# Two attention layers on one core: sums begun a unit earlier, six raw blocks in the last products, and outgoing tiles moved to band columns

## The chip, the core and the metric

The kernel runs on one core of one Trainium2 chip. A core has a matrix engine (TensorE; PE in the profile, with its weight loads shown apart as PEld), VectorE (DVE), ScalarE (ACT), GpSimd (POOL) and SyncE (SP), which here only issues DMAs. Each engine works through its own instruction list in order and waits for the others by semaphores. The matrix engine writes to PSUM; VectorE and ScalarE read PSUM and SBUF; transfers between the large memory (HBM) and SBUF run on sixteen DMA engines, and are issued here by SP, ACT and POOL. The metric is the device time of one execution in microseconds (us), lower is better.

## The reference

Two independent attention layers, each with 2048 positions of width 1024, 32 heads of 32, and fp32 inputs; the two outputs stand side by side.

```python
def _A_ref(x, wqkv, wo):          # layer A: 8 keys per query, every second position
    W, dil = 8, 2
    ...
    idx = pos[:, None] - (jnp.arange(W) * dil)[None, :]
    logits = einsum("bhsd,bhswd->bhsw", q, k[idx]) * scale     # masked where idx < 0
    o = einsum("bhsw,bhswd->bhsd", softmax(logits), v[idx])
    return o.reshape(B, S, D) @ wo

def _B_ref(x, wqkv, wo):          # layer B: a sliding window of 256 keys
    mask = (i - j >= 0) & (i - j < 256)
    o = softmax(where(mask, q @ k.T * scale, -1e9)) @ v
    return o.reshape(B, S, D) @ wo

out = concatenate([_A_ref(...), _B_ref(...)], axis=-1)
```

## The kernel before

**Units.** The work is cut into eight units of 512 positions. Units 0 to 3 are layer B, units 4 to 7 layer A ("the first to the fourth unit of layer A"; the odd and even positions of layer A are laid apart first, so its window is eight neighbours). A unit has eight head groups `s` of four heads; `hg = 8 * unit + s` numbers them through, so layer A has 32 to 63. For each head group the gemm of queries and keys runs (`qk_items`, L577), in some groups a block of the value gemm (`v_items`, L645), then the attention itself: in layer A `window`, with its scores (L914), a chain of mask, maximum, exponential and sum on DVE and ACT, a transposition (L952) into columns 1024 and up of a tile `band`, copies of those into a tile `wide` on ACT (L961, L964), and the product with the values (L975). There are two `band` tiles, taken by `hg` even and odd. `finish` copies the result to an SBUF slot and, in layer A, SP stores it to a DRAM tile `od` (L1028).

**fp32 through three products.** The matrix engine takes operands split in two parts, high and low. A block of 128 x 1024 floats (512 KB) arrives in a *raw* tile by a DMA that POOL issues (L169); ACT (L213) or DVE (L216) copies the high part out, DVE subtracts for the low part (L219); each 128 x 128 x 512 product then takes three matmuls.

**The stream of blocks.** `Stream` holds all blocks that are to be loaded, x and weights, in the order of their use (`items`). There are three raw tiles (`NRAW = 3`). When block `i` has been split, its raw tile is free and `load_to(i + 4)` asks for what lies up to three blocks ahead of the next. Some items have a *gate*: a test, in the planned time, that data which must exist first (`od`, `sd`, `td`, below) has been stored.

**The last products.** The output product of layer A isn't done unit by unit. Units 4 and 5, and 6 and 7, are two pairs, and each pair is multiplied with `wo` in seven products instead of eight (a Strassen-like scheme; the table `PRODUCTS`). All fourteen stand at the end of the gemm list (`product`, L764, 48 matmuls each: four groups `n` of twelve). A product needs two x-like blocks and two weight blocks, 512 KB each: some are `od` and `wo` themselves, others are sums, prepared ahead by `background` tasks: `weight_sums` makes `td` out of `wo`, and `output_sums(u, k)` makes `sd[u]` out of `od[u]` and `od[u + 1]`, in four tasks `k` for each pair. A task is two loads of 512 KB on SP's queue (L832), four additions on DVE (L837) and two stores of 512 KB on SP's queue (L843); it holds one of two lanes of SBUF slots. In the kernel before, the tasks of a pair are begun when head groups 4 to 7 of its second unit (unit 5, unit 7) have been stored. The product's additions out of PSUM are on DVE (L782), and its outputs are stored by ACT's queue (L787). The tile `o` that the second and the fifth product of a pair (`i` 1 and 4) send out is one of two room slots, the same as those that `finish` uses, or the tile `ost`.

**What sets the order.** While the program is being written, a small model (`Clock`) keeps the time at which each engine, queue and transfer would be done. A loop picks, from four lists (attention steps and gemm steps), the step that would be ready first, and writes it; deferred actions (evacuations, splits, loads, tasks) are written when the modelled time passes theirs. So every engine's list is fixed in that planned order, and a task that is begun at another place also shifts the modelled times of what comes after. SP's list has, in that order, the copies of layer A's queries and keys into their *seats* (`by_head`, L497: eight copies a head group, from a tile `nat` of a pool of three into one of two seats), the `od` stores and the tasks' loads and stores. The seats of `hg` are what its scores wait for; the model adds 4.0 us of slack to them (`SEAT_LATE`).

The functions that the diff touches, and what calls them:

Of the kernel before, what the change touches and what calls it, by code (L numbers as in the profile page):

```python
# [7 lines left out]
F32 = mybir.dt.float32  # L8
F32R = mybir.dt.float32r
# [5 lines left out]
P = 128  # L15
# [120 lines left out]
class Stream:  # L136
# [3 lines left out]
    def __init__(self, nc, ck, raws, wpool, xpool, items, more, light):  # L140

        self.nc, self.ck, self.raws, self.wpool, self.xpool, self.more = nc, ck, raws, wpool, xpool, more
        self.items = items
        self.raw, self.tiles, self.ready = {}, {}, {}
        self.loaded = self.split = self.wanted = 0
        self.gates = {}
        self.light = light
        self.load_to(NRAW + len(more))

    def load_to(self, n):  # L150
        while not self.loaded:
            self.raw = {i: (self.raws.tile([P, 1024], F32, tag="raw", name="raw"), []) for i in range(2)}
            for h in range(2):
                for i in range(2):
                    raw, t = self.raw[i]
                    ap = self.items[i][1]
                    self.nc.scalar.dma_start(raw[:, S * h:S * h + S], ap[:, h] if len(ap.shape) == 3 else ap[:, S * h:S * h + S])
                    t.append(self.ck.load("half", self.ck.now))
            self.loaded = 2
        self.wanted = max(self.wanted, n)  # L160
        while self.loaded < min(n, len(self.items)):
            gate = self.gates.get(self.loaded)
            if gate and not gate():
                return
            k = self.loaded - NRAW
            raw = self.more[k] if 0 <= k < len(self.more) else self.raws.tile([P, 1024], F32, tag="raw", name="raw")
            ap = self.items[self.loaded][1]
            early = k < len(self.more)
            (self.nc.scalar if early else self.nc.gpsimd).dma_start(raw if len(ap.shape) == 2 else raw.rearrange("p (a b) -> p a b", a=2), ap)  # L169
            self.raw[self.loaded] = raw, (self.ck.load if early else self.ck.fetch)("load", self.ck.now)  # L170
            self.loaded += 1

    def split_to(self, n):
        while not self.split:
            (rx, tx), (rw, tw) = self.raw.pop(0), self.raw.pop(1)
            self.tiles[0], self.ready[0], self.ready[1] = [], [], []
            w = self.tiles[1] = self.wpool.tile([P, 2, 1024], F32R, tag="w", name="w")
            for h in range(2):
                c = slice(h * S, h * S + S)
                self.tiles[0].append(self.xpool.tile([P, 2, S], F32R, tag="x", name="x"))  # L180
                self.ready[0].append(self.parts(self.tiles[0][h], rx[:, c], tx[h], True))
                self.ready[1].append(self.parts(w[:, :, c], rw[:, c], tw[h], True))
            self.split = 2
            for i in range(2):
                self.ck.defer(self.ready[i][1], lambda n=i + len(self.more) + NRAW + 1: self.load_to(n))
        while self.split < min(n, len(self.items)):
            i = self.split
            self.load_to(i + 1)
            if i not in self.raw:
                return  # L190
            raw, t0 = self.raw.pop(i)
            if self.items[i][0] != "w":
                self.tiles[i], self.ready[i] = [], []
                for h in range(2):
                    t = self.xpool.tile([P, 2, S], F32R, tag="x", name="x") if self.items[i][0] != "xw" else self.sums()
                    self.ready[i].append(self.parts(t, raw[:, h * S:(h + 1) * S], t0, i < SIDE))
                    self.tiles[i].append(t)
            else:
                t = self.wpool.tile([P, 2, 1024], F32R, tag="w", name="w")
                self.ready[i] = self.parts(t, raw, t0, i < SIDE)  # L200
                self.tiles[i] = t
            self.split += 1
            end = self.ready[i] if self.items[i][0] == "w" else max(self.ready[i])
            m = len(self.more)
            self.ck.defer(end, lambda n=i + m + NRAW + 1 if i < NRAW else max(2 * NRAW + m, i + NRAW + 1): self.load_to(n))

    def parts(self, t, raw, t0, side):

# [20 lines left out]
def kernel(ctx, tc, xs, wqk, wv, wo, outs, units):  # L229
# [51 lines left out]
    def landed(key, *which):  # L281
        return lambda: all(done[key].get(w, ck.now + 1) <= ck.now for w in which)
# [71 lines left out]
    def slot(i):  # L354
        return roomp.tile([P, 1024], F32, tag=f"r{i % NO}", name="r")
# [3 lines left out]
        return slot(4 + where_o["s"] % 4).rearrange("p (a s) -> p a s", a=2).bitcast(F32R)  # L359

    st.sums = sums_tile
    qst = [stackp.tile([P, 4, S], F32R, tag=f"q{i}", name=f"qst{i}") for i in range(2)]
    kst = [stackp.tile([P, 4, 256 + S], F32R, tag=f"k{i}", name=f"kst{i}") for i in range(2)]

# [47 lines left out]
    tails = const.tile([P, NG, 8], F32, name="tails")  # L412
    seats = more[:, :2 * (2 * S + 8)].rearrange("p (b c) -> p b c", b=2)
    band, wide = [None, None], [None, None]
    last_dense = sum(NG for u in units if u[2]) - 1
    halo = [[dram.tile([P, 2, 256], F32, name=f"halo{i}_{s}") for s in range(NG)] for i in range(2)]

    xt, xready, ot, rows, waiting = {}, {}, {}, {}, {}
# [315 lines left out]
    def product(u, i):  # L734
# [38 lines left out]
        def after(n, k):  # L773
            if k < 3:
                return
            ps, bank = h["ps"], h["b"]
            if i == 0 and n % 2 == 0:
                h["ac", n // 2] = [slot(8 + 2 * g + n // 2) for g in range(2)]
            a, c = [t[:, S * (n % 2):S * (n % 2) + S] for t in h["ac", n // 2]]

            def add(dst, src):
                nc.vector.tensor_tensor(dst, ps, src, op=ALU.add)  # L782
                return ck.use("dve", 0.61, ck.now + ck.SEM)

            def store(r, col, tile, e):
                def go():
                    nc.scalar.dma_start(outs[ORDER[u + r], 4 * col + n], tile)  # L787
                    ck.load("store", e)
                ck.defer(e, go)

            if i in (1, 4):
                where_o["ot"] += 1
                o = slot(2 + where_o["ot"] % 2)[:, :S] if where_o["ot"] % 3 else stp.tile([P, S], F32, tag="ost", name="ost")
            if i == 0:
                nc.scalar.copy(a, ps)
                e = ck.use("act", 0.485, ck.now + ck.SEM)
            elif i == 1:
                e = add(o, a)
                store(0, 0, o, e)
            elif i == 2:  # L800
                e = add(a, a)
            elif i == 3:
                e = add(c, a)
            elif i == 4:
                e = add(o, c)
                store(1, 0, o, e)
            elif i == 5:
                e = add(c, c)
                store(1, 1, c, e)
                e = add(a, a)  # L810
            else:
                e = add(a, a)
                store(0, 1, a, e)
            rg.give(bank, e)
# [53 lines left out]
    def output_sums(u, k):  # L868
        task([(2 * r, od[u + r][:, k::4, :]) for r in range(2)],
             ((3, 2, 3, ALU.add), (2, 0, 2, ALU.subtract), (0, 3, 0, ALU.subtract), (1, 1, 0, ALU.subtract)),  # L870
             sd[u][:, :, k, :], "s", (u, k))
# [146 lines left out]
    def finish(u, s, h):  # L1018
        hg = u * NG + s
        done["o"][hg] = ck.now  # L1020
        if u >= DU:
            o = slot(2 + hg % 2)[:, :S]
            nc.scalar.copy(o, h["o"])
            e = ck.use("act", 0.485, ck.now + ck.SEM)
            ro.give(0, e)

            def store():
                nc.sync.dma_start(od[u][:, s, :], o)  # L1028
                e2 = ck.copy("store", e)

                def end():
                    done["ot"][hg] = ck.now
                    st.load_to(st.wanted)
                    if s >= 4 and u % 2:
                        output_sums(u - 1, s - 4)

                ck.defer(e2 + 1.0, end)

            ck.defer(e, store)
            return  # L1040
        o = slot(hg).rearrange("p (a s) -> p a s", a=2).bitcast(F32R)
        ot[u, s] = o
        nc.scalar.copy(o[:, 0, :], h["o"])  # L1043
        r = ck.use("act", 0.485, ck.now + ck.SEM)

        def low():
            nc.vector.tensor_tensor(o[:, 1, :], h["o"], o[:, 0, :].bitcast(F32), op=ALU.subtract)  # L1047
            e = ck.use("dve", 0.61, r)
            ro.give(0, e)
            done["ot"][hg] = e  # L1050

        ck.defer(r, low)
# [292 lines left out]
```

## Time and profile before

| | |
|---|---|
| three runs | 1830.73 us median (1830.16 to 1833.35) |
| the profiled execution's own time | 1835.97 us |
| its span, from first to last instruction | 1834.0 us |
| mean granted TensorE clock | 0.991 |
| PE busy | 1799.3 us (98%) |
| DVE, ACT, POOL busy | 1262.2 (69%), 925.6 (50%), 409.2 us (22%) |
| matmuls of the last products (L764) | 672, 159.2 us busy, from 1662.6 us to the end |
| HBM read, written | 189.79 MB, 44.04 MB |

The page gives busy time by engine, the span in 40 slices, the DMA queues, the chain that ended last, and groups of instructions by line: a group's row has its busy time, the mean ns of one instruction, the idle time of the engine just before such instructions, and what ended most of that. In the order of time, a row has a start in us, a duration, engine, line, and in brackets the idle time before it and its releaser. SPq is SP's queue of instructions that issue DMAs. A table by stretches gives, for each window of the span, the busy us of each engine with the number of instructions, the granted clock (1.00 is full speed), the share of time in which the 16 DMA engines were busy, and GB/s.

### The profile page before, as it was taken

What the parts mean: (1) busy time and instruction counts of PE and PEld (TensorE: products, weight loads), DVE (VectorE), ACT (ScalarE), POOL (GpSimd) and SP (SyncE); (2) the same over time, 40 slices, a digit from 0 to 9 for tenths busy, and PEclk for the clock granted to TensorE, in tenths of its full rate; (3) what the DMA queues carried; (4) which work ended last, traced back from release to release, by engine and by line L of the source; (5) the groups of instructions that cost most, each with busy time, mean ns of one, the idle gap of its engine ahead of it and who ended that gap; (6) DMA issues with size and microseconds to landing.
All of it is one profiled execution on the core that took longest, in us unless ns stands there. A gap on an engine that the chain in (4) does not pass through costs nothing. (4 is left out here: it accounts for less than half of the span.)

```text
span 1834.0 us, 38630 instructions
## 1 busy us (share of the span) xinstructions
PE 1799.3 (98%) x14730; PEld 1467.6 (80%) x14730; DVE 1262.2 (69%) x2789; ACT 925.6 (50%) x2302; POOL 409.2 (22%) x950
## 2 busy tenths in 40 slices
PE   9999999999999999999999999999989999999999
PEld 7787777888778888777887788888868888787777
DVE  6777876778867669777777565655765665657666
ACT  4556466565656655656555344533533543435343
POOL 2312323223242323332233200110010011001111
PEclk9999999999999999999999999999989999999999
DMA  8455655645655556455554344547775455347886
GB/s 240 114 146 135 180 164 143 176 121 153 170 151 163 140 151 182 125 155 144 141 141 130 110 148 131 156 144 251 239 230 165 127 159 159 123 153 252 263 251 197
DMA packets 129241, 303.61 MB, mean 166 GB/s; under 512 B 16160, under 2 KB 31520, under 8 KB 129056
## 3 DMA queue, kind: packets, MB, share of 16 engines
q0 software_dynamic: 45216, 164.65, 30.6%
q1 hardware_dynamic: 73472, 116.56, 22.6%
q10 hardware_dynamic: 10368, 19.93, 3.0%
q8 instruction: 117, 1.92, 0.5%
q14 instruction: 68, 0.56, 0.1%
HBM read 189.79 MB, written 44.04 MB: 127 GB/s over the span
## 5 line engine op out<-in xcount | busy, mean ns | idle before, releaser
L577 PE MATMUL g<-x,w 128*128 128x512 f32 x3072 | 774.2, 396 | 6.2 <-ACT x L213 2.0
L577 PEld LDWEIGHTS g<-x,w 128*128 128x128 f32 x3072 | 567.2, 189 | 118.7 <-issue 6.8
L219 DVE TENSOR_TENSOR w<-raw,w 128x512 fp32r<-128x512 f32 x518 | 339.9, 698 | 87.7 <-ACT w L213 80.9
L645 PE MATMUL g<-w,x 128*128 128x256 f32 (+1 forms) x2304 | 396.6, 323 | 0.5 <-issue 0.3
L645 PEld LDWEIGHTS g<-w,x 128*128 128x128 f32 x2304 | 337.0, 192 | 29.6 <-issue 1.4
L1088 ACT ACTIVATE s<-s,nm 128x384 f32<-128x384 f32 (+2 forms) x512 | 274.4, 537 | 102.5 <-DVE nm L1083 102.3
L1083 DVE CUSTOM_DVE_ANT_0 s<-s,mask_d 128x384 f32<-128x384 f32 (+2 forms) x512 | 261.8, 554 | 88.2 <-PE s L1078 87.6
L1147 POOL TENSOR_SCALAR_AFFINE_SELECT pbuf<-pbuf 128x128 f32<-128x128 f32 (+1 forms) x606 | 219.3, 390 | 327.1 <-ACT pbuf L1168 325.8
L1168 ACT ACTIVATE pbuf<-s 128x384 f32<-128x384 f32 (+2 forms) x480 | 202.8, 505 | 73.9 <-PE s L1161 71.7
L705 PE MATMUL g<-r,w 128*128 128x512 f32 x768 | 190.8, 394 | 1.4 <-ACT r L1043 0.7
L169 POOL DMA_DIRECT2D raw<-wqk x126 | 68.2, 541 | 442.0 <-DVE w L219 296.9
L764 PE MATMUL g<-x,w 128*128 128x512 f32 x672 | 159.2, 397 | 7.5 <-ACT w L213 6.4
L705 PEld LDWEIGHTS g<-r,w 128*128 128x128 f32 x768 | 141.9, 188 | 30.8 <-DVE r L1047 1.6
L764 PEld LDWEIGHTS g<-x,w 128*128 128x128 f32 x672 | 127.2, 191 | 39.0 <-ACT w L213 8.1
L1161 PEld LDWEIGHTS s<-qst,kst 128*128 128x128 f32 x704 | 113.2, 189 | 40.9 <-ACT s L1088 16.2
L1078 PE MATMUL s<-kst,qst 96*128 96x384 f32 (+2 forms) x512 | 142.5, 342 | 1.0 <-ACT s L1088 0.7
L216 DVE CAST w<-raw 128x1024 fp32r<-128x1024 f32 x186 | 128.4, 691 | 21.6 <-PE g L577 17.6
L1161 PE MATMUL s<-qst,kst 128*128 128x256 f32 (+2 forms) x704 | 136.5, 302 | 3.5 <-ACT s L1088 3.0
L1078 PEld LDWEIGHTS s<-kst,qst 96*128 96x128 f32 x512 | 93.4, 188 | 26.1 <-issue 4.3
L922 DVE TENSOR_TENSOR band<-s,near 128x160 f32<-128x160 f32 x128 | 32.5, 317 | 111.1 <-PE s L914 111.1
L213 ACT CAST w<-raw 128x1024 fp32r<-128x1024 f32 (+1 forms) x74 | 76.4, 1037 | 61.6 <-DMA raw<-wo 22.8
L1088 ACT ACTIVATION_READ_ACCUMULATOR s<-s,nm 128x1 f32 x512 | 105.3, 206 | 0.0
(80 smaller groups left out, 1409.2 us busy)
## 6 DMA issues: line engine op xcount, KB each, us to landing
raw<-wqk POOLq DMA_DIRECT2D x126, 512.0 KB, 4.4
raw<-wv POOLq DMA_DIRECT2D x72, 512.0 KB, 4.9
qst<-nat SPq DMA_DIRECT2D x96, 256.0 KB, 4.8
kst<-nat SPq DMA_DIRECT2D x96, 256.0 KB, 5.7
raw<-wo POOLq DMA_DIRECT2D x44, 512.0 KB, 4.4
raw<-xs POOLq DMA_DIRECT2D x28, 512.0 KB, 4.7
outs<-ost ACTq DMA_DIRECT2D x37, 256.0 KB, 3.0
kst<-halo SPq DMA_DIRECT2D x72, 128.0 KB, 4.5
```

Source lines behind the costliest of these rows:

```text
L216: nc.vector.tensor_copy(t[:, 0, :], raw)
L219: nc.vector.tensor_tensor(t[:, 1, c:c + 512], raw[:, c:c + 512], t[:, 0, c:c + 512].bitcast(F32), op=ALU.subtract)
L577: nc.tensor.matmul(h["ps"], h["w"][:, a, k * P:(k + 1) * P], xt[u][k][:, b, :], start=(k == 0 and i == 0), stop=(k == NK - 1 and i == 2))
L645: nc.tensor.matmul(ps, xt[u][kw * g + k][:, a, p0:p0 + P], h["w"][g][:, c, k], start=(first and t == 0 and half == 0), stop=(last and t == 2),
L705: nc.tensor.matmul(h["ps"], w[:, a, c:c + P], ot[u, k][:, b, :], start=(k == 0 and i == 0), stop=(k == NK - 1 and i == 2))
L764: nc.tensor.matmul(h["ps"], w[:, a, c:c + P], x[:, b, :], start=(k == 0 and t == 0), stop=(k == 3 and t == 2))
L1078: nc.tensor.matmul(ps[:, :n], q[0:96, j, b * P:(b + 1) * P], kk[0:96, j, c0:c1], start=True, stop=True)
L1083: nc.vector.tensor_tensor_reduce(ps[:, :n], ps[:, :n], mask[:, cut:full], scale=-1.0, scalar=BIG, op0=ALU.add, op1=ALU.min, accum_out=nm)
L1088: nc.scalar.activation(ps[:, :n], ps[:, :n], AF.Exp, bias=nm, scale=-1.0, accum_out=sm)
L1147: nc.gpsimd.affine_select(w, w, pattern=[[0, m], [step, n]], compare_op=ALU.is_ge, fill=0.0, base=base, channel_multiplier=chan)
L1161: nc.tensor.matmul(ps[:, i * n:(i + 1) * n], kk[:, j, 256 + kb * P:256 + (kb + 1) * P], q[:, j, q0:q0 + n], start=True, stop=True)
L1168: nc.scalar.activation(w, ps[:, :pack * n].rearrange("p (j n) -> p j n", j=pack), AF.Exp)
```

## The change

- **Six raw blocks in turn.** `st.wide` is the first weight block of the first of the fourteen products. From this item on, three items go to tiles of the pool `nat` (its 1040 columns hold a block of 1024) and three to the raw tiles, alternately. From three items before `wide`, a block that has been split asks for loads three items further than before (`deep`). The first three items that go to `nat` tiles have gates: the seats of the last three head groups, which stand in these tiles, must have been copied in the planned time.
- **The sums of the first pair.** The four tasks of units 4 and 5 are begun when head groups 1 to 4 of unit 6 (the third of layer A) have been stored, rather than groups 4 to 7 of unit 5. Those of units 6 and 7 are begun where they were.
- **Outgoing tiles.** `o` is no longer a room slot but columns 1024 to 1535 of one of the two `band` tiles (by the same count, modulo two); each third is `ost` as before.

```diff
@@ class Stream
+        self.wide = len(items)
...
             k = self.loaded - NRAW
-            raw = self.more[k] if 0 <= k < len(self.more) else self.raws.tile([P, 1024], F32, tag="raw", name="raw")
+            if self.loaded >= self.wide and (self.loaded - self.wide) % (2 * NRAW) < NRAW:
+                raw = self.room()
+            else:
+                raw = self.more[k] if 0 <= k < len(self.more) else self.raws.tile([P, 1024], F32, tag="raw", name="raw")
...
-            self.ck.defer(end, lambda n=i + m + NRAW + 1 if i < NRAW else max(2 * NRAW + m, i + NRAW + 1): self.load_to(n))
+            deep = NRAW if i >= self.wide - NRAW else 0
+            self.ck.defer(end, lambda n=i + m + NRAW + 1 if i < NRAW else max(2 * NRAW + m, i + NRAW + deep + 1): self.load_to(n))
...
     st.sums = sums_tile
+    last_dense = DU * NG - 1
+    st.wide = where["p", DU, 0, "t", 0]
+    st.room = lambda: natp.tile([P, 2 * S + 16], F32R, tag="nat", name="raw").bitcast(F32)[:, :2 * S]
+    for i in range(NN):
+        gates[st.wide + i] = landed("nat", U * NG + last_dense + 1 - NN + i)
...
-    last_dense = sum(NG for u in units if u[2]) - 1
...
             if i in (1, 4):
                 where_o["ot"] += 1
-                o = slot(2 + where_o["ot"] % 2)[:, :S] if where_o["ot"] % 3 else stp.tile([P, S], F32, tag="ost", name="ost")
+                o = band[where_o["ot"] % 2][:, 1024:1536] if where_o["ot"] % 3 else stp.tile([P, S], F32, tag="ost", name="ost")
...
                     st.load_to(st.wanted)
-                    if s >= 4 and u % 2:
+                    if u == U - 1 and s >= 4:
                         output_sums(u - 1, s - 4)
+                    if u == U - 2 and 0 < s < 5:
+                        output_sums(DU, s - 1)
```

## The prediction

> **What bounds the kernel now.** The page comes first, with its row of busy times:
>
> ```profile
> PE 1799.3 (98%) x14730; PEld 1467.6 (80%) x14730; DVE 1262.2 (69%) x2789; ACT 925.6 (50%) x2302; POOL 409.2 (22%) x950
> ```
>
> PE is busy for 1799.3 of 1834.0 us, so at most some 35 us of idle matrix engine can be won, and beside it what a lower clock costs. Next comes the table of stretches of 40 us over layer A's last units and the products. Its columns are busy us of PE, PEld, DVE, ACT and POOL with counts, then the granted clock, the DMA share and GB/s.
>
> ```profile
> 1320.00:1360.00 40.00, 36.07 (x472) 30.07 (x471) 30.06 (x52) 20.28 (x38) 6.70 (x11) 0.96 0.73 229
> 1360.00:1400.00 40.00, 37.48 (x334) 29.87 (x333) 23.27 (x39) 10.00 (x18) 3.28 (x7) 0.91 0.68 223
> 1400.00:1440.00 40.00, 40.00 (x596) 32.70 (x595) 21.24 (x41) 18.03 (x34) 2.65 (x5) 1.00 0.40 125
> ...
> 1480.00:1520.00 40.00, 39.31 (x516) 33.76 (x515) 25.70 (x44) 20.64 (x39) 6.41 (x11) 1.00 0.53 157
> ...
> 1680.00:1720.00 40.00, 36.50 (x182) 28.98 (x181) 28.84 (x46) 16.67 (x26) 5.82 (x11) 0.93 0.78 254
> 1720.00:1760.00 40.00, 38.99 (x171) 31.54 (x170) 28.36 (x48) 14.24 (x21) 8.44 (x14) 1.00 0.86 266
> ```
>
> Lost PE time stands where the DMA share is 0.68 to 0.86; unit 6 from 1400 to 1440 loses nothing at a share of 0.40. The order of time on PE shows the single gaps. First the change from unit 5 to unit 6:
>
> ```profile
> 1337.46 3.93 PE L577 MATMUL g<-x,w 128*128 128x512 f32 x16
> 1342.23 1.43 PE L577 MATMUL g<-x,w 128*128 128x512 f32 x5 [0.84 <-DVE x L219]
> 1345.28 0.73 PE L577 MATMUL g<-x,w 128*128 128x512 f32 x2 [1.62 <-ACT w L213]
> 1347.48 3.04 PE L577 MATMUL g<-x,w 128*128 128x512 f32 x7 [1.47 <-DVE w L219]
> ...
> 1368.81 0.35 PE L914 MATMUL s<-pbuf 32*32 32x40 f32 x6 [2.44 <-issue]
> 1369.09 16.73 PE L645 MATMUL g<-w,x 128*128 128x512 f32 x60
> ```
>
> Then the end of unit 7 and the products, with the group's row of the page before it:
>
> ```profile
> L764 PE MATMUL g<-x,w 128*128 128x512 f32 x672 | 159.2, 397 | 7.5 <-ACT w L213 6.4
> ```
>
> ```profile
> 1605.97 0.65 PE L975 MATMUL o<-wide,vbuf 128*32 128x136 f32 x13 [2.58 <-issue]
> ...
> 1662.61 11.68 PE L764 MATMUL g<-x,w 128*128 128x512 f32 x48
> 1677.23 8.98 PE L764 MATMUL g<-x,w 128*128 128x512 f32 x30 [2.95 <-ACT w L213]
> ...
> 1687.25 15.52 PE L764 MATMUL g<-x,w 128*128 128x512 f32 x66
> 1706.27 39.96 PE L764 MATMUL g<-x,w 128*128 128x512 f32 x168 [3.50 <-ACT w L213]
> 1747.02 11.25 PE L764 MATMUL g<-x,w 128*128 128x512 f32 x48 [0.79 <-DVE r L782]
> 1758.49 71.82 PE L764 MATMUL g<-x,w 128*128 128x512 f32 x312 [0.23 <-DVE r L782]
> ```
>
> The last row is undisturbed: 312 matmuls in 71.82 us, the last of which takes 0.39, so (71.82 - 0.39) / 311 = 0.230 us from one to the next, and n of them should take 0.230 n + 0.16. By this the products lose 2.95 + 3.50 + 0.79 + 0.23 = 7.5 us idle, and the first four L764 rows run over by 0.5, 1.9, 0.2 and 1.2 = 3.7 us: together 11.2 us. The unit boundary loses 0.84 + 1.62 + 1.47 = 3.9 us idle and 1.6 us in slow rows (above all seven matmuls in 3.04 in place of 1.77): 5.5 us. So a gap draws 1.2 to 1.9 us of slow matmuls behind it (1.2, 1.3 and 1.9 here); I take 1.5 for a new one. The gap at 1366.4 (row 1368.81) has 2.44 us idle and 2.8 us of slow matmuls behind it: 5.2 us. That gap, and the 2.58 us before row 1605.97, are put down to "issue": the profile shows nothing that they wait for, so I can't say that the change removes them.
>
> **The first edit: six raw blocks.** No instruction is added: POOL issues the same 56 loads, four for each product, at other times. What the early loads wait for is read on POOL:
>
> ```profile
> 1670.11 0.72 POOL L169 DMA_DIRECT2D raw<-wo  x1 [5.36 <-ACT x L213]
> ...
> 1694.92 0.53 POOL L169 DMA_DIRECT2D raw<-td  x1 [1.27 <-issue]
> ```
>
> The first weight block of the second product is issued only at 1670.11, 5.36 us after POOL had nothing to do, when a raw tile came free; ACT splits it as it lands and PE waits until 1677.23. The block behind the wait that ends at 1706.27 (fourth product, a `td` block) is issued at 1694.92, and waits in a dense stretch of transfers:
>
> ```profile
> 1700.00:1705.00 5.00, 2.77 (x13) 1.96 (x11) 1.90 (x3) 1.14 (x2) 0.53 (x1) 1.00 1.01 375
> ```
>
> With loads asked for seven items ahead rather than four, the former goes out when the first x block of the first product has been split, about 1660; the latter when that of the third product has been, about 1687 (its splits stand at 1683.35 to 1686.12 in the rows of the third edit). Gains of some 10 and 8 us stand against gaps of 2.95 and 3.50 us, so both loads stop being what ends last. The new gates cost nothing by my reading: they hold the first three blocks until seats are copied that the last scores, which run before row 1662.61, need anyway, and the item under the latest gate belongs to the second product, 11 us behind that row. If a gate is closed longer, the old distance of loading is the upper bound: the gain is lost, and nothing more.
>
> What is late next? Faster products meet DVE. In the tail DVE waits for ACT's high parts, which wait for landings; those waits go, but a new one comes with the third edit, and is priced there. I keep 4.2 us of the 11.2 us: a bound of 0 below, 11.2 above, nearer to the former, since the rows name loads for 6.45 of the 7.5 us idle.
>
> On the clock the rows decide: seven matmuls after gaps of 0.84, 1.62 and 1.47 us, and 30 after one of 2.95 us, ran slow. [...]
>
> **The second edit: the sums.** Each of four tasks has two loads and two stores of 512 KB and four additions, 2 MB of transfers. At the boundary they collide with the x blocks of unit 6:
>
> ```profile
> 1325.00:1330.00 5.00, 5.00 (x44) 5.00 (x43) 4.31 (x7) 2.75 (x4) 1.34 (x3) 1.00 1.00 333
> 1330.00:1335.00 5.00, 5.00 (x44) 5.00 (x44) 0.97 (x2) 0.00 (x0) 0.24 (x1) 1.00 1.05 344
> ```
>
> ```profile
> 1338.71 2.87 DVE L837 TENSOR_TENSOR r<-r 128x512 f32<-128x512 f32 x4
> 1341.49 1.28 DVE L219 TENSOR_TENSOR x<-raw,x 128x512 fp32r<-128x512 f32 x2
> ...
> 1369.06 2.87 DVE L837 TENSOR_TENSOR r<-r 128x512 f32<-128x512 f32 x4 [7.90 <-DMA r<-od]
> ```
>
> DMA engines are full (1.00 and 1.05) just when x is loaded, and on DVE the four additions of a task (2.87 us) stand before the x split (1341.49) that ends the 0.84 us gap. Without the tasks 2 MB less move in these 10 us and 2.87 us of DVE come free. Row 1480 of the table shows a boundary without tasks (unit 6 to 7): it lost 0.69 us. I take that for what remains, so 4.8 of 5.5 us are won; the ends are 0 (the x blocks wait for raw tiles, not for transfers) and 5.5.
>
> In unit 6 the tasks begin behind the stores of head groups 1 to 4, about 1430 to 1480. The transfers fit: 8 MB over 50 us add 160 GB/s to the 125 of row 1400, a little more than rows 1320 and 1360 carry. On DVE, 11.5 us in 50 are added to a load of 21 in 40. On SP's list each task puts two loads and two stores between the seat copies; a store waits for the additions, and the seats behind it wait with it, for no longer than DVE does. On DVE the additions wait for the loads: row 1369.06 held DVE for 7.90 us. Who waits behind them is the window chain of that head group:
>
> ```profile
> 1407.57 1.32 PE L914 MATMUL s<-pbuf 32*32 32x40 f32 x128
> ...
> 1421.32 1.12 PE L975 MATMUL o<-wide,vbuf 128*32 128x136 f32 x32
> ```
>
> ```profile
> 1505.12 0.94 DVE band L922 x4
> ...
> 1507.76 0.62 DVE w L216
> ...
> 1508.40 1.30 DVE w L219 x2
> ...
> 1517.22 0.30 ACT wide L964
> ```
>
> In unit 6 the values start 12.4 us after the scores end (1408.89 to 1421.32). The chain of another head group, which was critical throughout, took 12.4 us from 1505.12 to 1517.52, 1.9 of them a split (1507.76 and 1508.40): 10.5 us net. So the slack is 1.9 us, and a longer hold of DVE stalls PE. The ends are 0 (the loads land in time at a DMA share of 0.4) and 4 x (7.9 - 1.9 + 1.5 of slow matmuls) = 30 us. I take 3 us, one task in four that stalls PE by 1.5 us and draws 1.5 of slow matmuls: near the lower end, because the long hold was at shares of 0.7 and more, which unit 6 doesn't have.
>
> **The third edit: outgoing tiles.** The first `o` is now in the `band` tile of the last head group, whose last copy on ACT (1685.15) must be through before DVE may write:
>
> ```profile
> 1682.75 0.68 DVE L782 TENSOR_TENSOR r<-g,r 128x512 f32<-128x512 f32 x1
> 1683.35 0.42 DVE L216 CAST x<-raw 128x512 fp32r<-128x512 f32 x1
> ...
> 1686.12 1.90 DVE L219 TENSOR_TENSOR x<-raw,x 128x512 fp32r<-128x512 f32 x3 [1.62 <-ACT x L213]
> ```
>
> ```profile
> 1685.15 0.29 ACT L964 COPY wide<-band 32x128 f32<-32x128 f32 x1
> ```
>
> The addition that ran at 1682.75 would wait for 1685.44: 2.7 us on DVE, with three splits of the third product behind it (1683.35 to 1686.12). PE has two more PSUM banks of twelve matmuls, 5.5 us, before it needs that addition, but the splits are due when product two ends. So up to 2.7 us idle and 1.5 of slow matmuls come back: these are the 4.2 us kept above; the other end is 0, if the last chain is through earlier because DVE no longer waits for landings. What it frees, the slots shared with `finish`, has no wait of the matrix engine to its name.
>
> **The sum.** Tail -11.2 + 4.2 = -7.0; boundary -4.8; unit 6 +3.0; "issue" gaps 0 (the ends are -10, both gone with their slow clock, and +10, two more of their kind when the order on PE moves). Together -8.8: the profiled execution, with 1834.0 us of span and 1835.97 in all, becomes 1827.2. It lies 5.2 us above the median of the runs, so the runs should go from 1830.73 to 1822.
>
> **The rivals.** *A, transfers and not blocks bound the tail.* The share is 0.78 and 0.86 in rows 1680 and 1720, and 1.01 at the second gap (row 1700); blocks asked for earlier then only land later, and the products keep their 11.2 us. Against it: row 1680 as a whole leaves a fifth of the DMA time, which earlier loads can use. Time: 1830.73 - 4.8 + 3.0 = 1829 at worst, 1826 if unit 6 is free; 1827. [...]
>
> *B, slower: the additions hold DVE in unit 6.* The place is the four window chains after 1430; it decides once a hold passes 1.9 us by enough that four of them exceed the other gains, 11.8 / 4 = 3.0 us of PE each, 1.5 of them idle: a hold of 3.4 us. For it speaks row 1369.06, against it the emptier DMA. With holds as long as that row, +30 in place of +3: 1849; with half of that excess, 4 x (3.0 + 1.5) = +18: 1837. I take 1837.
>
> *C, the change doesn't do what it says.* The x blocks wait for raw tiles that the splits on DVE release, the last products' splits are planned where they were, and the gaps move along: within 0.2% (3.7 us, about what a measurement of this kernel can tell from no change), 1830. For it, the longest sum in the table of waits from 1230 us on:
>
> ```profile
> POOL raw L169 <- DVE w L219: 273.6, 55, 18.7
> ```
>
> Against it: a POOL that waits has asked early, and in rows 1325 and 1330 it is the DMA engines that are full.
>
> **How the numbers follow.** My forecast 0.52 (its own range, from all of both gains and no cost at 1814 to half of the tail's gain at 1826); A 0.16; B 0.19; C 0.13. Faster: the forecast, A without the part at 1829 (0.13) and a little of C (0.03): 0.68. Slower: B and a little of C: 0.20. Same: 0.12. The range goes down to 1811 (an "issue" gap gone as well) and up to 1838, just past B; about 0.05 is left out below and 0.12 above.
>
> **What will show it.** Right: no idle above a microsecond before L764's first four products, wait rows of L764 on ACT's splits near 0 in place of 6.4; the sums' additions between 1420 and 1490; the boundary with under 1 us idle. Wrong: PE rows of L975 or L914 in unit 6 that wait for ACT's copies or the seats, with clock under 1.00; an addition L782 that waits for ACT's L964; loads that take 10 us and more to land in the products; new "issue" gaps, which move the time by 5 us each and say nothing on the theory.

## The result and the profile after

The changed kernel takes 1816.1 us (median of four runs, 1813.9 to 1820.48), against 1832.04 before in the same comparison: the ratio is 0.9916, with a 95% interval from 0.9892 to 0.9941. The forecast was faster, 1822 us within 1811 to 1838. The profiled execution took 1818.10 us, with a span of 1816.4, so its span is 17.6 us shorter than the one of before. Executions of one and the same kernel scatter (the four of the changed kernel lie 6.6 us apart, and the profiled one of the kernel before lies 5.2 us above the median of its runs), so differences of a few us between two profiled executions are no measure of an edit by themselves.

The sums of the first pair are begun later in the changed kernel than in the one before, not earlier as the title has it: behind head groups 1 to 4 of unit 6 in place of groups 4 to 7 of unit 5.

The line numbers have moved: L764 is L773 now, L577 is L586, L645 is L654, L914 is L923, L975 is L984, L782 is L791, L837 is L846, L169 is L173; L213, L216 and L219, the splits, are L218, L221 and L224; L952, L961 and L964, the transposition and the copies, are L961, L970 and L973. Kernels that are made out of the one before (e2, e3 and e5) keep the old numbers. First, of the page of the changed kernel, the busy times and the row of the last products:

```profile
PE 1789.4 (99%) x14730; PEld 1465.3 (81%) x14730; DVE 1262.0 (69%) x2790; ACT 924.4 (51%) x2301; POOL 410.1 (23%) x950
...
L773 PE MATMUL g<-x,w 128*128 128x512 f32 x672 | 153.2, 390 | 0.5 <-DVE w L224 0.5
```

The idle time before the products' matmuls has gone from 7.5 to 0.5 us. The order of time on PE, over the products:

```profile
1656.81 0.66 PE L984 MATMUL o<-wide,vbuf 128*32 128x136 f32 x16 [0.90 <-DVE vbuf L610]
1657.39 0.73 PE L773 MATMUL g<-x,w 128*128 128x512 f32 x2
1658.61 13.45 PE L773 MATMUL g<-x,w 128*128 128x512 f32 x58 [0.48 <-DVE w L224]
1671.98 1.42 PE L984 MATMUL o<-wide,vbuf 128*32 128x8 f32 x40
1673.33 139.04 PE L773 MATMUL g<-x,w 128*128 128x512 f32 x612
```

Of fourteen products, 612 matmuls run in one row without a gap: (139.04 - 0.39) / 611 = 0.227 us each. From the first to the last, 154.97 us pass, and 167.70 before. What the early blocks do is read on POOL:

```profile
1656.44 0.72 POOL L173 DMA_DIRECT2D raw<-wo  x1 [1.50 <-DVE x L224]
...
1675.72 0.53 POOL L173 DMA_DIRECT2D raw<-td  x1 [3.85 <-DVE x L224]
```

The first weight block of the second product goes out 0.95 us ahead of the first product (row 1656.44), where it was 7.5 us behind its start. The `td` block that held the fourth product goes out 18.3 us behind the start of the first (row 1675.72), where it was 32.3. The table of stretches, with the columns as before:

```profile
1360.00:1400.00 40.00, 40.00 (x448) 32.60 (x447) 19.53 (x36) 8.96 (x17) 3.17 (x6) 1.00 0.38 124
1400.00:1440.00 40.00, 40.00 (x599) 32.85 (x598) 28.68 (x52) 22.12 (x42) 3.18 (x6) 1.00 0.53 174
1440.00:1480.00 40.00, 40.00 (x548) 34.66 (x548) 28.13 (x48) 19.95 (x38) 3.17 (x6) 1.00 0.84 272
1480.00:1520.00 40.00, 36.94 (x374) 31.28 (x373) 26.92 (x43) 18.01 (x35) 6.80 (x11) 0.96 0.64 203
1680.00:1720.00 40.00, 40.00 (x178) 33.12 (x178) 31.94 (x52) 16.43 (x23) 7.30 (x14) 1.00 0.91 314
1720.00:1760.00 40.00, 40.00 (x178) 33.16 (x177) 28.81 (x48) 14.23 (x21) 9.32 (x16) 1.00 0.83 271
```

The DMA share over the products rose to 0.91 (row 1680) and PE idles nowhere in it: the transfers were not what they lacked. In unit 6 the sums now move data from 1430 to 1480 (272 GB/s in row 1440) without any idle matrix engine. The gaps that are left stand in the order of time on PE:

```profile
1343.38 1.12 PE L984 MATMUL o<-wide,vbuf 128*32 128x136 f32 x32 [1.09 <-ACT wide L973]
...
1490.92 0.33 PE L923 MATMUL s<-pbuf 32*32 32x40 f32 x23 [0.53 <-issue]
...
1500.88 1.50 PE L984 MATMUL o<-wide,vbuf 128*32 128x136 f32 x32 [2.54 <-ACT wide L973]
1502.32 6.95 PE L586 MATMUL g<-x,w 128*128 128x512 f32 x24
...
1599.64 0.64 PE L984 MATMUL o<-wide,vbuf 128*32 128x136 f32 x11 [2.55 <-issue]
```

The boundary of units 5 and 6 has one gap of 1.09 us where three made 3.9; that of units 6 and 7 has a new one of 2.54 us, and 24 matmuls behind it take 6.95 us where 24 x 0.227 + 0.16 = 5.6 would do. The "issue" gap of 1366 us is gone, the one of 2.6 us in unit 7 has stayed (row 1599.64).

So of the 17.6 us of span, 167.70 - 154.97 = 12.7 were won within the products, and 5.2 ahead of them, since the first product starts at 1657.39 and not at 1662.61; what follows the last matmul is 0.3 us longer. The 5.2 us are made up of -4.4 at the boundary of units 5 and 6 (5.5 to 1.1), -5.2 of the "issue" gap at 1366 with its slow matmuls, and 4.5 us of new gaps: 2.54 and 1.3 of slow matmuls less the 0.7 that this boundary lost before, and 0.53 and 0.90 elsewhere (rows 1490.92 and 1656.81). This part is one execution against another: in e9 below, which differs from the changed kernel only in where the outgoing tiles lie, the products begin at 1651.24, another 6 us earlier. The part within the products is firm, as the experiments show.

### The profile page after: what moved, and what is told of

Same layout as the page of the kernel before. It is cut to its first block, busy times and chain, and to the rows that moved or that the text cites. A ratio compares the mean times of both kernels' runs of the same rounds, so it can differ in the third digit from the quotient of the medians.

```text
span 1816.4 us, 38617 instructions
## 1 busy us (share of the span) xinstructions
PE 1789.4 (99%) x14730; PEld 1465.3 (81%) x14730; DVE 1262.0 (69%) x2790; ACT 924.4 (51%) x2301; POOL 410.1 (23%) x950
## 4 chain that ended last, share of the span: by engine, by line
PE 91%; DMA 3%; ACT 2%; DVE 2%; issue 1%; SPq 0%; POOL 0%; ACTq 0%; DVEq 0%; POOLq 0%
PE g L586 37%; PE g L654 18%; PE g L714 10%; PE g L773 8%; PE s L1172 5%; PE s L1089 5%; PE o L1219 5%; PE s L923 2%; PE o L984 2%; DMA r<-od 2%; DMA raw<-xs 1%; ACT wide L970 1%; ACT s L1099 0%; DVE w L224 0%; DVE r L846 0%
## 5 line engine op out<-in xcount | busy, mean ns | idle before, releaser
L586 PE MATMUL g<-x,w 128*128 128x512 f32 x3072 | 773.0, 396 | 2.8 <-ACT x L218 2.6
L586 PEld LDWEIGHTS g<-x,w 128*128 128x128 f32 x3072 | 568.1, 189 | 114.5 <-issue 6.8
L654 PE MATMUL g<-w,x 128*128 128x256 f32 (+1 forms) x2304 | 393.7, 322 | 0.5 <-issue 0.3
L224 DVE TENSOR_TENSOR w<-raw,w 128x512 fp32r<-128x512 f32 x518 | 339.4, 697 | 51.8 <-ACT w L218 45.1
L654 PEld LDWEIGHTS g<-w,x 128*128 128x128 f32 x2304 | 334.5, 192 | 28.8 <-issue 1.6
L173 POOL DMA_DIRECT2D raw<-wqk x126 | 68.6, 545 | 440.8 <-DVE w L224 303.0
L773 PE MATMUL g<-x,w 128*128 128x512 f32 x672 | 153.2, 390 | 0.5 <-DVE w L224 0.5
L773 PEld LDWEIGHTS g<-x,w 128*128 128x128 f32 x672 | 126.0, 188 | 27.3 <-DVE w L224 0.9
L221 DVE CAST w<-raw 128x1024 fp32r<-128x1024 f32 x187 | 129.3, 692 | 25.2 <-PE g L586 22.6
L970 ACT COPY wide<-band 32x512 f32<-32x512 f32 x128 | 79.0, 618 | 49.2 <-DVE band L961 47.2
```

Of the source, the lines that this page charges most:

```text
L221: nc.vector.tensor_copy(t[:, 0, :], raw)
L224: nc.vector.tensor_tensor(t[:, 1, c:c + 512], raw[:, c:c + 512], t[:, 0, c:c + 512].bitcast(F32), op=ALU.subtract)
L586: nc.tensor.matmul(h["ps"], h["w"][:, a, k * P:(k + 1) * P], xt[u][k][:, b, :], start=(k == 0 and i == 0), stop=(k == NK - 1 and i == 2))
L654: nc.tensor.matmul(ps, xt[u][kw * g + k][:, a, p0:p0 + P], h["w"][g][:, c, k], start=(first and t == 0 and half == 0), stop=(last and t == 2),
L773: nc.tensor.matmul(h["ps"], w[:, a, c:c + P], x[:, b, :], start=(k == 0 and t == 0), stop=(k == 3 and t == 2))
```

## The experiments

**Theory**: the products were short of raw tiles, and the collision of the sums with the x blocks of unit 6 made the gaps at that boundary; these are two independent gains, and the third edit gives nothing by itself. **Rivals**: the products were short of transfers, so that moving the sums freed them; the outgoing tiles' slots held them; and, for the first edit, two explanations: more tiles, or the earlier request. The kernels of one comparison share the runs of the kernel before: 1830.63 us for the first four, 1833.88 for the second four, 1830.62 for the last.

Three of the kernels (e3, e5, e6) have outgoing tiles in band columns, but loads asked for four items ahead. In the order in which they are written, the first outgoing tile then goes over columns that the copies of the last window have yet to read, so the last head group of layer A gets wrong numbers; the work is the same in amount.

**Each edit by itself.** The changed kernel with the sums begun in unit 5 again:

```diff
-                    if u == U - 1 and s >= 4:
+                    if s >= 4 and u % 2:
                         output_sums(u - 1, s - 4)
-                    if u == U - 2 and 0 < s < 5:
-                        output_sums(DU, s - 1)
```

> The changed kernel with the sums of the first pair begun in unit 5 again: six raw blocks and outgoing tiles in band columns alone. Theory (blocks, not transfers, held the products): the products need some 155 us from their first to their last matmul as in the changed kernel, against 167.7 before, so 12 to 13 us are won; the gaps at the change from unit 5 to unit 6 (5.5 us) and the 'issue' gap at 1366 us stay: about 1819.5 us. Rival (the products were short of transfers, and moving the sums freed them): the products keep at least half of their gaps, 1826 us or more.

Measured: 1822.52 us, ratio 0.9950 (0.9935 to 0.9965). The products take 154.98 us, as in the changed kernel to a hundredth, while the old gaps stand at the boundary of units 5 and 6 (order of time on PE):

```profile
1346.31 0.73 PE L586 MATMUL g<-x,w 128*128 128x512 f32 x2 [1.62 <-ACT w L218]
1348.53 3.35 PE L586 MATMUL g<-x,w 128*128 128x512 f32 x7 [1.48 <-DVE w L224]
```

The rival falls. The total is 3 us above my figure. The profiled spans (1834.0 and 1820.7) differ by 13.3 us, as the figure has it; the medians differ by less, since the profiled execution of the kernel before is one of its longer ones.

The kernel before with the sums moved, and nothing else (the same lines, the other way round):

> The kernel before with the sums of the first pair begun in unit 6, and nothing else. Theory: the boundary from unit 5 to 6 loses 1 us rather than 5.5, the one from 6 to 7 gets the new gap of 2.5 us with its slow matmuls, the 'issue' gap at 1366 us goes because the order on PE moves; the products keep their 11 to 14 us of loss: 1823 to 1829 us. Rival: 1818 or less, if the sums were also what held the products.

Measured: 1825.56 us, ratio 0.9968 (0.9955 to 0.9981). The two old waits of the products are there, at the same places of the work:

```profile
1665.55 8.98 PE L764 MATMUL g<-x,w 128*128 128x512 f32 x30 [1.98 <-ACT w L213]
...
1694.84 41.08 PE L764 MATMUL g<-x,w 128*128 128x512 f32 x168 [3.36 <-ACT w L213]
```

They take 170.0 us. Their start is at 1651.35, 11 us earlier than before: the boundary and the gap at 1366 us are won, and lost again in part. The sums neither made nor removed the products' waits.

The kernel before with the outgoing tiles in band columns:

```diff
-                o = slot(2 + where_o["ot"] % 2)[:, :S] if where_o["ot"] % 3 else stp.tile(...)
+                o = band[where_o["ot"] % 2][:, 1024:1536] if where_o["ot"] % 3 else stp.tile(...)
```

> The kernel before with the outgoing tiles in band columns, and nothing else. Theory: DVE's first addition waits up to 2.7 us for the copies of the last window, which costs the matrix engine 0 to 4 us; nothing is won: 1831 to 1836 us. Rival: the room slots shared with the stores of layer A held the products, and 4 us or more are won: 1828 or less.

Measured: 1834.08 us, ratio 1.0016 (1.0003 to 1.0029), the products 167.7 us. The edit gives nothing by itself. Whether it can be left out is not shown: by my reading of the lists, with six raw tiles and the old room slots engines would wait for each other in a circle, and no run has that combination. And the changed kernel without the six tiles, sums and band columns alone:

> The changed kernel without the six raw blocks (three raw tiles, loads asked for four items ahead): sums in unit 6 and outgoing tiles in band columns. Theory: the products lose 11 to 14 us again, and the time is that of the sums alone, 1823 to 1829 us. Rival (the sums or the tiles did it): 1818 or less.

Measured: 1824.45 us, ratio 0.9951 (0.9933 to 0.9969), the products 168.0 us. It agrees with e2, as the theory has it. By the ratios, blocks and band columns (e1) give 0.50% or 9.2 us, the sums alone (e2) 0.32% or 5.9 us, and the whole change 0.84% or 15.4 us: the two gains add up within their intervals.

**More tiles, or an earlier request?** The changed kernel with the old distance:

```diff
-            deep = NRAW if i >= self.wide - NRAW else 0
+            deep = 0
```

> The changed kernel with six raw tiles in turn, but loads still asked for when the block four items before has been split, as in the kernel before. Theory (it is the distance of the request that counts; the tile itself is what the old distance waits for): the loads go out as late as with three tiles, the products lose most of their 11 to 14 us again: 1824 to 1829 us. Rival (the loads waited for a raw tile's release on the chip and not for the place of the request in the program): half of the gain or more stays, 1820 or less.

Measured: 1818.54 us, ratio 0.9917 (0.9893 to 0.9941), the products 156.5 us. My theory falls, and the rival holds: the gain stays whole with the old distance. POOL's list of instructions is the same, row for row, in this program and the changed one: it has the loads in the same order however early the program asks for them, and each waits on the chip for its tile. From 1640 us on the list holds nothing but these loads, so there is no other work that an earlier request could overtake. What the distance does change is the place of other steps. DVE and ACT in this kernel:

```profile
1671.91 1.25 DVE L961 STREAM_TRANSPOSE band<-band 128x1024 f32<-128x1024 f32 x1
...
1674.67 0.69 DVE L791 TENSOR_TENSOR band<-g,r 128x512 f32<-128x512 f32 x1 [0.34 <-PE g L773]
```

```profile
1675.39 0.62 ACT L970 COPY wide<-band 32x512 f32<-32x512 f32 x1 [2.86 <-DVE band L791]
```

The first outgoing tile (L791, row 1674.67) is written between the transposition (L961) and the copies of what it made (L970). In the changed kernel the addition comes behind the last copy, after a wait of 1.44 us:

```profile
1672.26 0.69 DVE L791 TENSOR_TENSOR band<-g,r 128x512 f32<-128x512 f32 x1 [1.44 <-ACT wide L973]
...
1683.67 0.69 DVE L791 TENSOR_TENSOR band<-g,r 128x512 f32<-128x512 f32 x1 [2.65 <-DMA outs<-band]
```

To have this without the overwriting, the next two kernels put `o` into 512 columns of each of the tiles of `wide` that nothing uses:

```diff
         k = stackp.tile([P, 4, 256 + S], F32, tag=f"k{buf}", name="wide")
+        spare[buf] = k.rearrange("p j s -> p (j s)")[:, 4 * 544:4 * 544 + S]
...
-                o = band[where_o["ot"] % 2][:, 1024:1536] if where_o["ot"] % 3 else stp.tile(...)
+                o = spare[where_o['ot'] % 2] if where_o["ot"] % 3 else stp.tile(...)
```

With these columns and `deep = 0`:

> Six raw tiles in turn, loads asked for four items ahead as in the kernel before, outgoing tiles in the unused columns. Theory now (POOL's list has the loads in the same order however early the program asks, and each waits on the chip for the release of its tile alone): the products keep the whole gain, 154 to 158 us, total within 3 us of the changed kernel. Rival (the distance of the request counts): 165 us or more for the products, 1824 or more in total.

Measured: 1814.97 us, ratio 0.9917 (0.9896 to 0.9939), the products 154.8 us. Six tiles with the old distance have the whole gain. The other half, three tiles with the new distance (`if False:` in place of the test that takes a `nat` tile):

> Three raw tiles, loads asked for seven items ahead, outgoing tiles in the unused columns, sums in unit 6: the distance alone. Theory now: nothing of the products' gain, 164 us or more from their first to their last matmul, total 1823 to 1829 us. Rival: 1820 or less.

Measured: 1825.14 us, ratio 0.9972 (0.9959 to 0.9986), the products 167.6 us, with gaps spread over their first half:

```profile
1666.15 4.59 PE L773 MATMUL g<-x,w 128*128 128x512 f32 x12 [2.40 <-ACT w L218]
...
1699.27 5.70 PE L773 MATMUL g<-x,w 128*128 128x512 f32 x24 [1.51 <-DVE r L791]
...
1729.84 5.99 PE L773 MATMUL g<-x,w 128*128 128x512 f32 x24 [1.21 <-ACT w L218]
```

So for the products the distance does nothing, and the number of tiles does everything: six tiles need 155.0 us with the new distance (e9) and 154.8 with the old, three need 167.6 with the new (e11) and 167.7 to 170.0 with the old (the kernel before, e2, e3 and e5). All nine kernels with six tiles lie between 154.8 and 156.5 us. By the medians of one comparison, e9 and e11 differ by 12.7 us. With six tiles PE runs on (e10):

```profile
1654.16 17.52 PE L773 MATMUL g<-x,w 128*128 128x512 f32 x76 [0.48 <-DVE w L224]
...
1672.73 134.98 PE L773 MATMUL g<-x,w 128*128 128x512 f32 x594
```

**What the band columns cost.** The changed kernel with the unused columns:

> The changed kernel with the outgoing tiles in columns that nothing else uses (512 unused columns of each of the two tiles that hold wide) in place of the band columns, so that no addition waits for the last window's copies or for a transposition. Theory (the new waits of DVE on the band tiles, 1.4 and 4.2 us, lie in its idle time): the same time as the changed kernel within 3 us, products 154 to 156 us. Rival (the band tiles cost what I predicted, 2.7 us idle and 1.5 slow): 3 to 4 us faster.

Measured: 1812.48 us, ratio 0.9909 (0.9885 to 0.9932), the products 154.98 us against 154.97. The waits on the band tiles cost PE nothing within the products; between the two kernels the measurement shows no difference (0.9916 and 0.9909, each within the other's interval).

**The new gap at the boundary of units 6 and 7.** In the changed kernel ACT waits there for x blocks, 4.68 and 2.14 us, while the last sum is stored, and the window's exponential (L947) and its copies (L970, L973) stand behind these splits:

```profile
1486.93 1.14 ACT L218 CAST x<-raw 128x512 fp32r<-128x512 f32 x2 [4.68 <-DMA raw<-xs]
1490.20 1.14 ACT L218 CAST x<-raw 128x512 fp32r<-128x512 f32 x2 [2.14 <-DMA raw<-xs]
1491.25 0.74 ACT L947 ACTIVATE band<-band 128x640 f32<-128x640 f32 x1
```

The sums one head group earlier:

```diff
-                    if u == U - 2 and 0 < s < 5:
-                        output_sums(DU, s - 1)
+                    if u == U - 2 and s < 4:
+                        output_sums(DU, s)
```

> The changed kernel with the sums begun one head group earlier (behind head groups 0 to 3 of unit 6). Theory (the new gap of 2.54 us at the change from unit 6 to 7 is made by the last sum's stores beside the x blocks): that gap and its 1.5 us of slow matmuls go, the tasks now stand clear of both boundaries: 1811 to 1813 us beside 1816. Rival (that gap comes from the window's own chain behind the x splits): the gap stays, 1815 to 1817.

Measured: 1815.14 us, ratio 0.9911 (0.9896 to 0.9926). The gap of 2.54 us is down to 0.38, with 0.87 ahead of it, and e1, with the sums in unit 5, has 0.20 there, so the sums did make it; but no time is won beside the changed kernel's 0.9916:

```profile
1494.78 1.14 PE L586 MATMUL g<-x,w 128*128 128x512 f32 x3 [0.87 <-DVE w L221]
1496.30 1.12 PE L984 MATMUL o<-wide,vbuf 128*32 128x136 f32 x32 [0.38 <-ACT wide L973]
```

```profile
1652.69 0.66 PE L984 MATMUL o<-wide,vbuf 128*32 128x136 f32 x16 [2.10 <-DVE vbuf L610]
```

Another wait has grown in its place, at the last values product ahead of the products: 2.10 us for a value block (L610), 0.90 in the changed kernel. Why DVE copies that block later here stays open.

**The "issue" gaps.** I counted PE's instructions (matmuls, weight loads, semaphore instructions) in the order of their start. In all fourteen kernels the gaps of more than 0.5 us (from start to start) that are put down to "issue" from 1100 us on stand where the count is 193 modulo 256. PE's 29,903 instructions in the changed kernel over the 117 packets of queue q8, 16 KB each and marked "instruction" on the page, make 255.6 a packet; that these packets are PE's is my estimate from that number. So I shifted the list, with small matmuls behind the warming ones:

```diff
         for i in range(WARM):
             nc.tensor.matmul(ps, idle[:, :P], idle, start=True, stop=True)
+        for i in range(16):                              # 64 in the second
+            nc.tensor.matmul(ps[:, :32], idle[:, :P], idle[:, :32], start=True, stop=True)
```

> The changed kernel with 16 matmuls of 32 columns (32 instructions with their weight loads) behind the warming ones at the start, which fills no time that PE isn't idle in. All 'issue' gaps of both traces lie where the count of PE's instructions is 193 modulo 256. Theory (PE's code comes in blocks of 256 instructions, and a block that is worked off within a burst of small matmuls makes it wait for the next): the gap of 2.55 us in unit 7 at 1597 us goes or moves by 32 instructions to an earlier matmul, others may come: 1812 to 1820 us. Rival (the gap belongs to its place in the work): it stays at the same values product, 2.5 us long.

> As the run with 32 more instructions, but 64 small matmuls, 128 instructions, half a block. Theory: every 'issue' gap of the changed kernel disappears from its matmul, since its block border now lies 128 instructions away; gaps can only stand where the count is 193 modulo 256 again: 1810 to 1818 us. Rival: the gaps at 1118, 1158, 1491 and 1597 us stay where they are.

```
gaps of PE with the cause "issue", over 0.5 us from start to start: at us, count, us
changed kernel      1117.9 15041 0.63; 1157.9 16065 1.61; 1490.9 24257 0.73; 1599.6 26817 2.83
32 more (e7)        1285.3 18881 1.95; 1427.8 22465 1.86; 1490.3 24257 0.56
128 more (e8)       1294.6 18881 3.50; 1310.7 19393 0.63; 1470.4 23489 3.13; 1537.9 25025 1.93; 1586.9 26049 0.68
each count = 193 modulo 256
```

With 32 more the run takes 1813.89 us, ratio 0.9896 (0.9874 to 0.9917); the gap in unit 7 is gone, and two new ones are in units 5 and 6:

```profile
1592.59 1.31 PE L923 MATMUL s<-pbuf 32*32 32x40 f32 x128
1593.84 1.19 PE L984 MATMUL o<-wide,vbuf 128*32 128x8 f32 x40
```

```profile
1285.32 0.41 PE L984 MATMUL o<-wide,vbuf 128*32 128x128 f32 x2 [1.68 <-issue]
```

The rival falls: the gaps keep their count and not their place in the work. With 128 more it takes 1826.60 us, ratio 0.9968 (0.9953 to 0.9984). That the small matmuls would take no time was wrong for 64 of them:

```profile
5.96 13.67 PE L1282 MATMUL s<-qst 128*128 128x32 f32 x64
```

They take 13.67 us (its cause stays open, and a price per matmul is not shown), and forty matmuls further on PE is 9 us later than in the changed kernel; the gaps of up to 3.5 us come on top.

What stands near such a gap can be read in the traces, from the times of q8's packets. The longest of the changed kernel lies around a packet that runs from 1597.18 to 1598.07, and PE goes on at 1599.64, 1.57 us later. From 1100 us on the changed kernel and the one before have eight gaps of more than 0.5 us at counts of 193 modulo 256: each of them ends 1.21 to 1.57 us after the end of a q8 packet, while of the 116 such counts without a gap three have a packet's end 1.2 to 1.6 us ahead. What PE waits for in these gaps is not shown, nor why some counts have one: in these two kernels 256 instructions that ran in 1.57 us had no gap behind them, and others of 1.35 to 3.52 us had one.

**All together** (early sums, 32 more instructions, unused columns):

> The changed kernel with three more edits: sums behind head groups 0 to 3 of unit 6, 16 small matmuls (32 instructions) behind the warming ones, outgoing tiles in the unused columns. If the gains add up (gap at the boundary of units 6 and 7 gone, the 'issue' gap of 2.55 us in unit 7 gone): 1810 to 1813 us. If the block borders of PE's code fall into other bursts, since the order on PE has changed as well: 1814 to 1818 us.

Measured: 1816.62 us, ratio 0.9922 (0.9903 to 0.9941). The gains don't add up, as the second reading had it: an "issue" gap of 3.39 us has come in unit 6. No version tried is clearly faster than the changed kernel; the lowest ratios, 0.9896 and 0.9909, have intervals that overlap with its own.

## Why the prediction was right

The direction and the range held; the gain was 15.9 us by the medians (17.6 by the spans) where 8.8 was forecast. By its steps:

- **The boundary** (-4.8 us): -4.4 measured, and e1 and e2 show that the sums made the old gaps.
- **The tail** (-11.2 + 4.2 = -7.0 us): this term was mis-sized, with 12.7 us measured. First, the row of 312 matmuls that I took as undisturbed wasn't: its pace of 0.230 us is 0.227 in the changed kernel (seven of its matmuls start 0.31 to 0.41 us after the one ahead), so the products lost 167.7 - 1.2 - 672 x 0.227 = 14.0 us, not 11.2. Second, I kept 4.2 us for the wait on the band tile. DVE did wait, 1.44 us at the addition named, and 2.65 us at a later one for the store of a band tile, but the waits lie in DVE's slack, as e9 shows. I had seen that the PSUM banks give 5.5 us, and then charged the splits behind the addition all the same.
- **Why the tail gains**: the step "with loads asked for seven items ahead rather than four" was wrong. A load goes out when its tile is released, and the request's place in the program alters nothing on POOL's list (e10 and e11). The six tiles alone do it; the prediction took tiles and distance together and so couldn't tell which of them it needed.
- **Unit 6** (+3.0): no idle time at all from 1360 to 1480. DVE was held by the sums' loads three times:

```profile
1430.75 2.87 DVE L846 TENSOR_TENSOR r<-r 128x512 f32<-128x512 f32 x4 [0.50 <-DMA r<-od]
...
1448.49 2.87 DVE L846 TENSOR_TENSOR r<-r 128x512 f32<-128x512 f32 x4 [1.79 <-DMA r<-od]
...
1470.97 2.87 DVE L846 TENSOR_TENSOR r<-r 128x512 f32<-128x512 f32 x4 [4.25 <-DMA r<-od]
```

The longest hold, 4.25 us, is above the 1.9 us of slack that I had worked out, and yet PE didn't wait: no window chain was under way on DVE just then. The cost came in a place I had not priced, the boundary of units 6 and 7: 2.54 us and 1.3 of slow matmuls, where 0.7 was lost before. About the size, by another mechanism: that is luck. The 285 GB/s that were expected in unit 6 are also more than "a little" above the 229 and 223 of the old boundary; row 1440 reached 272, and it did no harm there.
- **The "issue" gaps** (0, between -10 and +10): the one at 1366 us went, 5.2 us with its slow matmuls, and that isn't shown to be a merit of the sums as such: moving them also changes the order on PE, and in e7 such gaps kept to their counts and not to their places in the work. By the terms of the prediction the sums give 4.8 - 3.0 = 1.8 us, and by e2 they give 5.9: that gap is most of the difference, and it is luck as well.
- **Rival A** (transfers bound the tail): fell. The DMA share rose from 0.78 to 0.91 with no gap. **Rival B**: fell, above. **Rival C**: fell; its reason, that POOL waits for releases, was the true bound of the products, and is what the six tiles relieve.
- **The clock**: the rows were right that gaps of the lengths they show can draw slow matmuls. Behind the new gap of 2.54 us the 24 matmuls of row 1502.32 took 1.3 us too long, at a granted clock of 0.81 from 1502.3 to 1509.2 us; the gap of 1.09 us drew none to speak of, with the clock at 1.00 from 1342.2 to 1352 us. But in these runs the length of a gap didn't decide by itself, so the 1.5 us that I took for each new one is no more than a middle value. At the same place of the work, 24 matmuls that should take 5.6 us took 7.35 behind 2.13 us in e5, and 5.74 behind 2.65 us in e11:

```profile
1496.33 1.12 PE L975 MATMUL o<-wide,vbuf 128*32 128x136 f32 x32 [2.13 <-ACT wide L964]
1497.38 7.35 PE L577 MATMUL g<-x,w 128*128 128x512 f32 x24
```

```profile
1498.09 1.12 PE L984 MATMUL o<-wide,vbuf 128*32 128x136 f32 x32 [2.65 <-ACT wide L973]
1499.14 5.74 PE L586 MATMUL g<-x,w 128*128 128x512 f32 x24
```

## What to carry to other kernels

Where a queue holds nothing but loads in a fixed order and each waits for its tile, count the tiles against the time from request to release, and don't look to the place of the request in the program: here six tiles with the old distance took 154.8 us (e10), three with the new one 167.6 (e11). A row that looks undisturbed is a poor measure of pace if it has small gaps in it: take the fastest long row of the same shape (here 0.227 us a matmul, and not 0.230). A transfer-heavy task that can be done anywhere belongs clear of the places where blocks are urgent; here that meant one unit later, and 4.4 us less lost at the boundary of units 5 and 6.

## What the runs showed of the hardware

The gaps of more than 0.5 us from 1100 us on that the profile puts down to "issue" stood at counts of 193 modulo 256 of PE's instructions in all fourteen kernels, and kept to such counts when 32 or 128 instructions were added in front (e7, e8), so that they moved against the work. In the changed kernel and the one before each of them ended 1.21 to 1.57 us after the end of a 16 KB packet of queue q8; what PE waited for is not shown. Such a gap took 0.5 to 3.8 us from start to start. Some had slow matmuls behind them: 2.8 us of them behind 2.44 us idle at 1366 us in the kernel before, at a granted clock of 0.50 from 1368.8 to 1374 us. That gap (5.2 us with what it drew) is a difference between the kernel before and the changed one at which no edit aimed. Padding wasn't free: 64 matmuls of 32 columns took 13.67 us at the start of e8.
